# A gated linear attention and a star-ReLU feed-forward on one core: another order of the opening, and w_in cast in other pieces

## The chip, the cores and the metric

The kernel runs on one core of one Trainium2 chip. The metric is the device time of one execution in microseconds. Before the change three runs gave 196.47, 197.56 and 197.69 us; the median is 197.56.

## The reference

Two layers one after the other. The first is a recurrence over 768 steps for each of 4 batches and 8 heads, with a state of 48 by 48; the second takes its output, with the heads put side by side, as 3072 tokens of width 384.

```python
for t in range(S):                         # q, k, v, alpha: (4, 8, 768, 48)
    state = alpha[:, :, t, :, None] * state + einsum('bhd,bhe->bhde', k[:, :, t], v[:, :, t])
    y[:, :, t] = einsum('bhd,bhde->bhe', q[:, :, t], state)
x = y.transpose(0, 2, 1, 3).reshape(3072, 384)
h = x @ w_in                               # w_in: (384, 2048)
g = s * maximum(h, 0) ** 2 + b
out = g @ w_out                            # w_out: (2048, 384), out: (3072, 384) float32
```

## The kernel before

The 3072 tokens are cut into 24 blocks of 128, six to each batch. A block n goes through these steps, each a small function:

- `load(n)`: four DMAs on SP's queue, alpha, k, q, v, in this order, 192 KB each.
- `ln(n)` (L189, ACT): the logarithm of alpha, written to `la_sb`. `vcast(n)` (L192, POOL): v to bf16.
- `cum(n)`: the running sum of the logarithms as a matmul with a triangle of ones (L198, and four narrow ones, L201, for the total), and on ACT the exponentials `bi_sb` (L209), `b_sb` (L210) and `blast` (L212).
- `qk(n)` (DVE): `kb_sb` = k times `bi_sb` (L226) and `qb_sb` = q times `b_sb` (L227).
- `tr(n)`: eight transposes on PE (L232) and one copy by DVE to `qkT` (L237).
- `amat(n)`: eight matmuls (L247) give the scores within the block, and DVE masks them into `am_a` and `am_b` (L255).
- `yp(n)`: the output of the block from the state (`sd_sb`, L266) and from the scores (L275), the state's increment (L286), and on ACT the copy `y_bf` (L293). `st(n)`: the state's update, one DVE instruction (`t_sb`, L337 or L339) and two or three on POOL (L344, L348).
- `xt(n)`: three transposes of `y_bf` (L317) and ACT's copy into `xd_all` (L323).
- `mr(g, u)`: one 512-wide piece of the first matrix product of group g (L365) and its relu on ACT into a ring of eight buffers `r_sb` (L379). `sq(g, u)` (L386, DVE) squares it into `gt_all`. Group 0 holds blocks 0 and 1, so its pieces cover 256 columns of w_in; group 1 is block 2, group 2 is block 3, and their pieces cover 512 columns.
- `o(n, u)`: a quarter of the second product (L403).

Weights arrive as float32 and are cast on the chip. `win(i)` casts a quarter of w_in's 2048 columns in three instructions, one for each 128 rows: `cast_w_in(c0, c1, act)` gives the first `act` of them to ACT (L140) and the others to DVE (L142). `wout(i)` casts a quarter of w_out and multiplies it by s, on DVE (L146) or, for i = 1, on ACT (L154). `busy(n)` issues n matmuls whose result nobody reads (L179). `colsum` and `bias_sum` work on the bias.

Nothing is reordered by a scheduler. `at(pos, fn, ...)` collects the steps, and they are issued in the order of their positions; every engine takes its instructions in that order. The opening, up to block 4's `amat`, is a list written out by hand, which takes positions in steps of 0.1; the rest follows from formulas. SP's queue begins with the loads of blocks 0 to 3, then the four quarters of w_in, the four of w_out, and the loads of blocks 4 to 7. `cum` of the first four blocks writes the PSUM bank `h_ps[1]`, `xt` of the first three `h_ps[0]`; the first pieces of `mr` go round five banks.

Of the kernel before, what the change touches and what calls it, by code (L numbers as in the profile page):

```python
# [14 lines left out]
def kernel(  # L15
# [122 lines left out]
    def cast_w_in(c0, c1, act=1):  # L138
        for kk in range(act):
            nc.scalar.activation(out=w_in_bf[:, kk, c0:c1], in_=w_in_st[:, kk, c0:c1], func=AF.Copy)  # L140
        for kk in range(act, KT):
            nc.vector.tensor_copy(out=w_in_bf[:, kk, c0:c1], in_=w_in_st[:, kk, c0:c1])  # L142
# [307 lines left out]
    quarter = d_ff // 4  # L450
# [24 lines left out]
    def at(pos, fn, *args):  # L475
        events.append((pos, len(events), fn, args))
# [5 lines left out]
    def wout(i):  # L482
        cast_w_out(4 * i, 4 * i + 4, i == 1)

    def win(i):
        cast_w_in(i * quarter, (i + 1) * quarter, 2 if i == 0 else 1)

    def m(g, u):
        mp(g, u)
# [10 lines left out]

    for pos, what in enumerate(
        [
            (ln, 0), (vcast, 0), (cum, 0), (qk, 0), (spread,), (busy, 3), (tr, 0), (ln, 1), (busy, 1), (vcast, 1), (cum, 1), (amat, 0),
            (busy, 3), (yp, 0), (qk, 1), (st, 0), (busy, 1), (tr, 1), (xt, 0), (ln, 2), (busy, 2), (vcast, 2), (cum, 2), (amat, 1),
            (busy, 3), (yp, 1), (qk, 2), (st, 1), (busy, 1), (tr, 2), (xt, 1), (ln, 3), (busy, 2), (vcast, 3), (cum, 3), (amat, 2),
            (busy, 3), (yp, 2), (qk, 3), (st, 2), (busy, 1), (tr, 3), (xt, 2), (busy, 3), (amat, 3), (win, 0), (busy, 4), (yp, 3),
            (mr, 0, 0), (mr, 0, 1), (xt, 3), (mr, 1, 0), (win, 1), (sq, 0, 0), (mr, 0, 2), (mr, 0, 3), (mr, 1, 1), (win, 2), (sq, 0, 1),
            (sq, 1, 0), (mr, 2, 0), (mr, 2, 1), (win, 3), (st, 3), (sq, 0, 2), (sq, 0, 3), (mr, 0, 4), (mr, 0, 5), (wout, 0), (mr, 1, 2),
            (sq, 1, 1), (sq, 2, 0), (mr, 2, 2), (sq, 2, 1), (mr, 0, 6), (sq, 0, 4), (o, 0, 0), (wout, 1), (mr, 0, 7), (sq, 0, 5),
            (o, 1, 0), (mr, 1, 3), (sq, 1, 2), (o, 2, 0), (mr, 2, 3), (sq, 2, 2), (sq, 0, 6), (wout, 2), (sq, 0, 7), (o, 0, 1), (sq, 1, 3),  # L510
            (o, 1, 1), (sq, 2, 3), (ln, 4), (wout, 3), (o, 2, 1), (cum, 4), (o, 0, 2), (vcast, 4), (qk, 4), (o, 1, 2), (o, 2, 2), (colsum, 1),
            (o, 0, 3), (o, 1, 3), (tr, 4), (o, 2, 3), (o, 3, 0), (colsum, 2), (amat, 4),
        ]
    ):
        at(0.1 * pos, *what)
# [64 lines left out]
```

## Time and profile before

| | |
|---|---|
| runs | 196.47, 197.56, 197.69 us |
| profiled execution | 196.55 us, its span 194.8 us |
| PE busy | 180.9 us, 93% of the span |
| DVE, ACT, POOL busy | 150.5, 119.5, 61.4 us |
| DMA | 30.31 MB, mean 156 GB/s |
| costliest lines on PE | L365 71.1 us, L403 68.3 us |
| costliest line on ACT | L379 53.5 us |

The span is what the profiler saw on the core; the execution's own time is 1.75 us longer. "Idle before, and its releaser" names the time in which an engine stood still and the instruction that let it go on; on an engine that is not the bound such time costs nothing. Times in a timeline are in us from the span's start. Starts of successive instructions on one engine can be closer than their durations, because they overlap.

### The profile page before, as it was taken

To read this page: it belongs to the slowest core of one execution; us is meant where nothing else is said; L and a number is where in the kernel's file an instruction comes from. 1 tells how busy PE (TensorE), PEld (TensorE's weight loads), DVE (VectorE), ACT (ScalarE), POOL (GpSimd) and SP (SyncE) were. 2 spreads that over 40 slices of the span, in tenths; PEclk is the share of its full clock that TensorE was granted. 3 is DMA by queue.
4 is the path that set the end of the run, shared out by engine and by line. 5 is a ranking of instruction groups with operands and counts; after the bars stand their busy time and mean duration, and the time that the engine had idled before them with its cause. 6 is when DMAs were issued, how large, how long until landed. Compare 5 with 4: busy or idle time off the path is not lost.

```text
span 194.8 us, 6003 instructions
## 1 busy us (share of the span) xinstructions
PE 180.9 (93%) x2389; PEld 143.3 (74%) x2391; DVE 150.5 (77%) x294; ACT 119.5 (61%) x245; POOL 61.4 (32%) x96
## 2 busy tenths in 40 slices
PE   1977879999999999999999999999999999999994
PEld 1544459866777788778878888888877877877783
DVE  5367778657687788888887996878988988998532
ACT  3344567953677666766677676775675566654640
POOL 5154404021310515624500641642401565352000
PEclk9999999999999999999999999999999999999999
DMA  6999999999996484484958448759886948433212
GB/s 126 188 185 190 359 388 371 233 192 188 186 156 108 71 155 88 80 150 82 173 91 162 83 85 162 131 80 198 165 175 149 216 117 166 128 120 121 84 40 81
DMA packets 113453, 30.31 MB, mean 156 GB/s; under 512 B 106627, under 2 KB 111890, under 8 KB 113426
## 3 DMA queue, kind: packets, MB, share of 16 engines
q1 hardware_dynamic: 113422, 29.94, 74.3%
q8 instruction: 18, 0.29, 0.7%
q14 instruction: 9, 0.07, 0.1%
q10 hardware_dynamic: 4, 0.00, 0.0%
HBM read 25.19 MB, written 4.74 MB: 154 GB/s over the span
## 4 chain that ended last, share of the span: by engine, by line
PE 80%; DVE 4%; ACT 3%; issue 1%; ACTq 0%
PE h_ps L365 29%; PE o_ps L403 28%; PE ct_ps L232 5%; PE a_ps L247 3%; PE a_ps L403 3%; PE y_ps L275 2%; ACT r_sb L379 2%; PE h_ps L317 2%; PE ct_ps L198 2%; PE a_ps L426 1%; PE p_ps L286 1%; PE y_ps L266 1%; DVE gt_all L386 1%; DVE w_out_bf L146 1%; DVE am_b L255 1%
## 5 line engine op out<-in xcount | busy, mean ns | idle before, releaser
L379 ACT ACTIVATE r_sb<-h_ps 128x512 bf16<-128x512 f32 x90 | 53.5, 597 | 35.5 <-PE h_ps L365 33.2
L365 PEld LDWEIGHTS <-w_in_bf 128*128 128x128 bf16 x1104 | 67.9, 98 | 8.0 <-ACT w_in_bf L140 1.4
L365 PE MATMUL h_ps<-xd_all,w_in_bf 128*128 128x128 bf16 (+1 forms) x1044 | 71.1, 221 | 0.1
L403 PE MATMUL o_ps<-w_out_bf,gt_all 128*128 128x384 bf16 x336 | 68.3, 326 | 0.1
L386 DVE TENSOR_TENSOR gt_all<-r_sb 128x512 bf16<-128x512 bf16 x96 | 45.1, 482 | 26.5 <-ACT r_sb L379 25.8
L344 POOL TENSOR_TENSOR sd_sb<-t_sb,blast 48x192 bf16<-48x192 f32 x40 | 20.1, 503 | 91.8 <-DVE t_sb L339 53.9
L403 PEld LDWEIGHTS <-gt_all 128*128 128x128 bf16 x368 | 32.6, 98 | 16.0
L192 POOL CAST v_bf<-v_sb 128x384 bf16<-128x384 f32 x24 | 17.0, 712 | 24.2 <-DMA v_sb<-in_v_dram 20.7
L348 POOL TENSOR_TENSOR sc_sb<-t_sb,blast 112x384 f32<-112x384 f32 x16 | 22.0, 1372 | 1.3
L323 ACT ACTIVATE xd_all<-h_ps 128x384 bf16<-128x384 bf16 x23 | 11.3, 491 | 15.6 <-PE h_ps L317 15.6
L237 DVE COPY qkT<-ct_ps 112x1024 bf16<-112x1024 bf16 x24 | 16.4, 683 | 4.5 <-PE ct_ps L232 3.0
L255 DVE TENSOR_TENSOR am_a<-a_ps,mask 128x512 bf16<-128x512 f32 x24 | 16.4, 683 | 4.2 <-PE a_ps L247 4.1
L226 DVE TENSOR_TENSOR kb_sb<-k_sb,bi_sb 128x384 bf16<-128x384 f32 x24 | 13.8, 574 | 4.5 <-ACT bi_sb L209 4.5
L255 DVE TENSOR_TENSOR am_b<-a_ps,mask 128x512 bf16<-128x512 f32 x24 | 16.3, 680 | 0.0
L227 DVE TENSOR_TENSOR qb_sb<-q_sb,b_sb 128x384 bf16<-128x384 f32 x24 | 16.0, 668 | 0.0
L293 ACT ACTIVATE y_bf<-y_ps 128x384 bf16<-128x384 f32 x24 | 11.7, 489 | 5.6 <-PE y_ps L275 5.6
L189 ACT ACTIVATE la_sb<-al_sb 128x384 bf16<-128x384 f32 x24 | 12.4, 516 | 3.9 <-DMA al_sb<-in_alpha_dram 3.9
L232 PEld LDWEIGHTS <-qb_sb 128*112 128x112 bf16 x96 | 8.3, 133 | 5.3 <-DVE qb_sb L227 4.1
L209 ACT ACTIVATE bi_sb<-ct_ps 128x384 f32<-128x384 f32 x20 | 9.7, 486 | 2.3 <-PE ct_ps L201 1.3
L232 PE MATMUL ct_ps<-ident,qb_sb 128*112 128x128 bf16 x96 | 9.9, 227 | 0.9 <-DVE qb_sb L227 0.9
L210 ACT ACTIVATE b_sb<-ct_ps 128x384 f32<-128x384 f32 x20 | 9.9, 495 | 0.0
L275 PE MATMUL y_ps<-v_bf,am_b 128*128 128x48 bf16 x96 | 8.1, 184 | 1.7 <-DVE am_b L255 1.7
(75 smaller groups left out, 200.9 us busy)
## 6 DMA issues: line engine op xcount, KB each, us to landing
al_sb<-in_alpha_dram SPq DMA_DIRECT2D x24, 192.0 KB, 4.1
k_sb<-in_k_dram SPq DMA_DIRECT2D x24, 192.0 KB, 4.0
q_sb<-in_q_dram SPq DMA_DIRECT2D x24, 192.0 KB, 4.4
v_sb<-in_v_dram SPq DMA_DIRECT2D x24, 192.0 KB, 5.2
w_in_st<-in_moe_w_in_dram SPq DMA_DIRECT2D x4, 768.0 KB
w_out_st<-in_moe_w_out_dram SPq DMA_DIRECT2D x4, 768.0 KB, 12.8
out_dram<-w_in_st SPq DMA_DIRECT2D x14, 192.0 KB, 2.0
out_dram<-out_sb SPq DMA_DIRECT2D x9, 192.0 KB
```

What stands on the lines that cost most here:

```text
L192: nc.gpsimd.tensor_copy(out=v_bf[n % 3], in_=v_sb[n % NLD])
L226: nc.vector.tensor_tensor(out=kb_sb[n % 3][:, :, 0:48], in0=k_sb[n % NLD], in1=bi_sb[n % 2], op=ALU.mult)
L227: nc.vector.tensor_tensor(out=qb_sb[n % 2][:, :, 0:48], in0=q_sb[n % NLD], in1=b_sb[n % 3], op=ALU.mult)
L232: nc.tensor.transpose(out=t_ps[0:112, x, p, :], in_=t.rearrange("a h d -> a (h d)")[:, 128 * p : 128 * p + 112], identity=ident,)
L237: nc.vector.tensor_copy(out=qkT_sb[n % 2][0:112].rearrange("a x p t -> a (x p t)"), in_=t_ps[0:112].rearrange("a x p t -> a (x p t)"),)
L255: nc.vector.tensor_tensor(out=am_sb[e][n % 2], in0=a_ps[e], in1=mask4, op=ALU.mult)
L344: nc.gpsimd.tensor_tensor(out=sd[r, :, d], in0=t1_sb[r, :, d], in1=bl[r].to_broadcast([48, NP, 48]), op=ALU.mult)
L348: nc.gpsimd.tensor_tensor(out=sc_sb[0:112], in0=t1_sb[0:112], in1=bl[0:112].to_broadcast([112, NP, 96]), op=ALU.mult)
L365: nc.tensor.matmul(out=hp[:, jj * N : (jj + 1) * N], lhsT=w_in_bf[:, kk, 128 * j : 128 * (j + 1)], rhs=xd_sb[g][:, kk, 0:N], start=(kk == ...
L379: nc.scalar.activation(out=rs, in_=h_of.pop((g, u)), func=AF.Relu)
L386: nc.vector.tensor_tensor(out=gt_sb[g][:, u * 512 : (u + 1) * 512], in0=rs, in1=rs, op=ALU.mult)
L403: nc.tensor.matmul(out=op[:, 0:d_model], lhsT=gt_sb[g][:, j * N + t * C : j * N + (t + 1) * C], rhs=w_out_bf[:, j, :], start=(j == 0), sto ...
```

## The change

The list of the opening is written anew, and `win` works on units of 256 columns.

- `busy` ahead of `tr(0)` has two matmuls instead of three; the two ahead of `cum(2)` and of `cum(3)` become one, placed behind it; the four ahead of `yp(3)` become three.
- `amat(0)` is placed ahead of `cum(1)`.
- `ln(2)` is placed ahead of `xt(0)`, and `ln(3)` ahead of `xt(1)`.
- `win(i)` casts 256 columns with all three instructions on ACT; `win(i, 2)` casts 512, one instruction on ACT and two on DVE. The first quarter becomes `win(0)` ahead of `yp(3)` and `win(1)` behind it. The other three stay 512 wide and are placed among the first pieces of `mr`: the first of them between `mr(0,0)` and `mr(0,1)`, the next between `mr(0,2)` and `mr(0,3)`, the last between `mr(2,0)` and `mr(2,1)`.
- `ln(4)` and `cum(4)` are placed some steps earlier (`cum(4)` ahead of `o(2,1)`), and `tr(4)` ahead of `o(1,3)`.

On the engines: ACT has six casts of 256 columns and three of 512 instead of five of 512; DVE has six casts instead of seven; PE has four matmuls and their weight loads fewer; the orders of DVE, POOL and SP are otherwise the same.

```diff
-    def win(i):
-        cast_w_in(i * quarter, (i + 1) * quarter, 2 if i == 0 else 1)
+    def win(i, n=1):
+        cast_w_in(i * 256, (i + n) * 256, 3 if n == 1 else 1)
...
-            (ln, 0), (vcast, 0), (cum, 0), (qk, 0), (spread,), (busy, 3), (tr, 0), (ln, 1), (busy, 1), (vcast, 1), (cum, 1), (amat, 0),
-            (busy, 3), (yp, 0), (qk, 1), (st, 0), (busy, 1), (tr, 1), (xt, 0), (ln, 2), (busy, 2), (vcast, 2), (cum, 2), (amat, 1),
-            (busy, 3), (yp, 1), (qk, 2), (st, 1), (busy, 1), (tr, 2), (xt, 1), (ln, 3), (busy, 2), (vcast, 3), (cum, 3), (amat, 2),
-            (busy, 3), (yp, 2), (qk, 3), (st, 2), (busy, 1), (tr, 3), (xt, 2), (busy, 3), (amat, 3), (win, 0), (busy, 4), (yp, 3),
-            (mr, 0, 0), (mr, 0, 1), (xt, 3), (mr, 1, 0), (win, 1), (sq, 0, 0), (mr, 0, 2), (mr, 0, 3), (mr, 1, 1), (win, 2), (sq, 0, 1),
-            (sq, 1, 0), (mr, 2, 0), (mr, 2, 1), (win, 3), (st, 3), (sq, 0, 2), (sq, 0, 3), (mr, 0, 4), (mr, 0, 5), (wout, 0), (mr, 1, 2),
+            (ln, 0), (vcast, 0), (cum, 0), (qk, 0), (spread,), (busy, 2), (tr, 0), (ln, 1), (busy, 1), (vcast, 1), (amat, 0), (cum, 1),
+            (busy, 3), (yp, 0), (qk, 1), (st, 0), (busy, 1), (tr, 1), (ln, 2), (xt, 0), (vcast, 2), (cum, 2), (busy, 1), (amat, 1),
+            (busy, 3), (yp, 1), (qk, 2), (st, 1), (busy, 1), (tr, 2), (ln, 3), (xt, 1), (vcast, 3), (cum, 3), (busy, 1), (amat, 2),
+            (busy, 3), (yp, 2), (qk, 3), (st, 2), (busy, 1), (tr, 3), (xt, 2), (busy, 3),
+            (amat, 3), (win, 0), (busy, 3), (yp, 3), (win, 1),
+            (mr, 0, 0), (win, 2, 2), (mr, 0, 1), (xt, 3), (mr, 1, 0), (sq, 0, 0), (mr, 0, 2), (win, 4, 2), (mr, 0, 3), (sq, 0, 1), (mr, 1, 1),
+            (sq, 1, 0), (mr, 2, 0), (win, 6, 2), (mr, 2, 1), (st, 3), (sq, 0, 2), (sq, 0, 3), (mr, 0, 4), (mr, 0, 5), (wout, 0), (mr, 1, 2),
             (sq, 1, 1), (sq, 2, 0), (mr, 2, 2), (sq, 2, 1), (mr, 0, 6), (sq, 0, 4), (o, 0, 0), (wout, 1), (mr, 0, 7), (sq, 0, 5),
-            (o, 1, 0), (mr, 1, 3), (sq, 1, 2), (o, 2, 0), (mr, 2, 3), (sq, 2, 2), (sq, 0, 6), (wout, 2), (sq, 0, 7), (o, 0, 1), (sq, 1, 3),
-            (o, 1, 1), (sq, 2, 3), (ln, 4), (wout, 3), (o, 2, 1), (cum, 4), (o, 0, 2), (vcast, 4), (qk, 4), (o, 1, 2), (o, 2, 2), (colsum, 1),
-            (o, 0, 3), (o, 1, 3), (tr, 4), (o, 2, 3), (o, 3, 0), (colsum, 2), (amat, 4),
+            (o, 1, 0), (mr, 1, 3), (sq, 1, 2), (o, 2, 0), (mr, 2, 3), (sq, 2, 2), (sq, 0, 6), (ln, 4), (wout, 2), (sq, 0, 7), (o, 0, 1),
+            (sq, 1, 3), (o, 1, 1), (sq, 2, 3), (cum, 4), (wout, 3), (o, 2, 1), (o, 0, 2), (vcast, 4), (qk, 4), (o, 1, 2), (o, 2, 2),
+            (colsum, 1), (o, 0, 3), (tr, 4), (o, 1, 3), (o, 2, 3), (o, 3, 0), (colsum, 2), (amat, 4),
```

## The prediction

> **What bounds the kernel now.** I read the page first: shares, slices, releasers.
>
> ```profile
> span 194.8 us, 6003 instructions
> PE 180.9 (93%) x2389; PEld 143.3 (74%) x2391; DVE 150.5 (77%) x294; ACT 119.5 (61%) x245; POOL 61.4 (32%) x96
> ...
> PE   1977879999999999999999999999999999999994
> ...
> PEclk9999999999999999999999999999999999999999
> ```
>
> PE is busy 93% of the span, and only the first six slices of 4.87 us and the last show gaps. So microseconds can be won in the opening alone, and what the opening gains the end gets, because from there on PE's own work sets the pace. The table of stretches confirms it (columns: stretch, its length, busy us and instructions of PE, PEld, DVE, ACT, POOL, then PEclk, DMA share, GB/s):
>
> ```profile
> 14.00:19.00 5.00, 3.71 (x47) 2.42 (x46) 3.51 (x6) 2.33 (x6) 2.28 (x5) 1.00 1.30 182
> 26.00:28.00 2.00, 2.00 (x27) 1.78 (x24) 1.11 (x5) 1.67 (x4) 0.00 (x0) 1.00 1.05 400
> 28.00:30.00 2.00, 0.76 (x9) 0.64 (x8) 1.91 (x6) 1.25 (x3) 0.00 (x0) 1.00 1.06 377
> 32.00:36.00 4.00, 3.87 (x55) 3.53 (x53) 3.67 (x7) 4.00 (x9) 0.59 (x1) 1.00 1.07 360
> 100.00:150.00 50.00, 49.88 (x701) 41.16 (x700) 42.70 (x81) 33.74 (x71) 15.15 (x20) 1.00 0.72 132
> ```
>
> Blocks 1 to 3 take about 5 us each, PE idle for over a quarter of it and filled with dummy matmuls besides. At 28 to 30 us PE is idle for 1.24 us. At 100 to 150 us it idles for 0.12 of 50.
>
> Then the timeline of the opening, for what each gap waits on (start, us, engine, line, operation; in brackets the idle time before and what ended it):
>
> ```profile
> 16.48 0.55 DVE L227 TENSOR_TENSOR qb_sb<-q_sb,b_sb 128x384 bf16<-128x384 f32 x1
> ...
> 17.77 0.69 DVE L237 COPY qkT<-ct_ps 112x1024 bf16<-112x1024 bf16 x1 [0.28 <-PE ct_ps L232]
> 17.94 0.49 ACT L323 ACTIVATE xd_all<-h_ps 128x384 bf16<-128x384 bf16 x1 [1.05 <-PE h_ps L317]
> ...
> 18.32 0.52 ACT L189 ACTIVATE la_sb<-al_sb 128x384 bf16<-128x384 f32 x1
> ...
> 18.89 0.32 PE L198 MATMUL h_ps<-la_sb,U_bf 128*128 128x384 bf16 x1 [0.56 <-ACT la_sb L189]
> ...
> 19.30 0.40 PE L247 MATMUL a_ps<-qkT 48*128 48x128 bf16 x8
> ```
>
> This is block 2. Its qkT is done at 18.46, yet its amat (L247) starts at 19.30. In PE's order it stands behind cum(3), which waits for ln(3), which stands on ACT behind the copy of xt(1). Block 1 is the same (xt copy 12.87, ln 13.26, cum 13.82, amat 14.24). The second gap:
>
> ```profile
> 28.61 0.64 ACT L140 ACTIVATE w_in_bf<-w_in_st 128x512 bf16<-128x512 f32 x1
> ...
> 29.30 0.83 PE L365 MATMUL a_ps<-xd_all,w_in_bf 128*128 128x256 bf16 x6 [1.24 <-ACT w_in_bf L140]
> ```
>
> Here mr(0,2) waits for ACT's part of the cast of the second quarter of w_in, which stands behind two relus, the copy of xt(3) and a third relu.
>
> **When the data lands.** Moving work earlier pays only up to its load, so I need landings that the trace mostly hides. In the first 16 us a load lands 4.7 us after its issue starts: al(1) 3.52 to 8.24, v(1) 6.69 to 11.42, v(2) 10.94 to 15.64, each ending an idle wait. By that, al(2) lands at 7.72+4.7=12.4, al(3) at 16.7, k(3) 17.7, q(3) 18.75. v(3) is seen at 20.75. A quarter of w_in or w_out is 0.786 MB, 2.1 us at 377 GB/s, so counted from 20.75 the quarters of w_in land at 22.8, 24.9, 27.0, 29.0 and those of w_out at 31.1, 33.2, 35.3, 37.4. Before, their casts began at 23.43, 25.6, 27.6, 29.1 and 31.83 without idling: consistent, and upper bounds. Then 0.197 MB a load at 190 GB/s, 1.03 us: al(4) 38.4, k(4) 39.5, q(4) 40.5, v(4) 41.6; v(4) ended a wait at 41.72. SP's order is unchanged and waits for no compute here, so landings stay.
>
> **The change, part by part.**
>
> *ln ahead of xt, amat ahead of cum(1).* One block's circle, by start times of block 2: am_a to kb 1.20 (14.67, 15.87), kb to qb 0.61, qb to transposes 0.60, to qkT 0.69, to the earliest amat 0.75 (22.87, 23.62), to am_a 0.43: 4.28 us instead of 5.06. Block 0: amat no longer waits for cum(1), 7.97+0.75=8.72 instead of 9.23. am_a 9.2, kb(1) 10.4 (bi(1), now behind amat, at 10.2), qb(1) 10.85 (q(1) landed at 10.3; one step 0.46 as at 10.94 and 11.40), transposes 11.45, qkT 12.15. ln(2) waits for al(2): 12.4 to 12.92, cum(2) 12.97. From cum to amat 0.42 (13.82, 14.24), and one dummy matmul that now stands between, 0.22: amat(1) 13.6, for 14.24. Two stood ahead of cum, inside its wait, so dropping them gives nothing. The copy of xt(0) moves behind ln(2), but PE finishes that transpose about then anyway. Block 2: 13.6+4.28=17.9 for the qkT, and 17.2+0.05+0.64=17.9 by ln(3): amat(2) 17.9, for 19.30. Block 3: 22.2, for 23.62. v(3) is cast by 21.25 and sd(2) follows on POOL to 22.35, in time for yp(3). Gain 1.42, and mr(0,0) starts at 25.75-1.42=24.33. If al(2) and al(3) landed only where ln started before (13.26, 18.32), the dummy between would cost 0.22 a block, in all -0.2: these are the two ends. I take 1.42, since 4.7 us was seen three times.
>
> *win(0) and win(1) in halves, all on ACT.* ACT pieces of 512 and 384 start 0.52 and 0.385 apart back to back; by that slope 256 takes 0.25. Three from 22.8 end at 23.65, hidden behind amat(3) and yp(3); even from 23.43 they end at 24.3, just in time. win(1) follows the y_bf copy (24.42): 24.8 to 25.66. mr(0,0) ends at 24.98, so PE waits 0.7 for mr(0,1) at 25.7: this is the new wait, priced in. DVE loses one cast of 0.42 behind am_b(3), which bounded nothing.
>
> *The later casts.* On ACT win(2,2) now stands ahead of the second relu: done 26.6 against mr(0,2) at 27.2. The next, done by 29.0 and 31.0, come before mr(0,4) and mr(0,6). So the 1.24 us gap goes. From 25.7 PE has 11 groups of 0.67 and one transpose of 0.17 up to mr(0,6): 33.25, for 35.61. ACT needs the same time (relu 0.48, cast 0.52): done with relu(1,2), which frees mr(0,6)'s bank, at 32.95. w_out's first cast ends by 31.15+1.58=32.7, o(0,0) needs it at 33.95. Gain so far 2.36: 1.42 and 1.24 and 0.4 of smaller waits, less 0.7.
>
> *ln(4), cum(4), tr(4) earlier.* cum(4) moves ahead of o(2,1), to 42.16-2.36-0.65=39.15. relu(2,3) ends at 38.55 and al(4) lands at 38.4, so la is ready at 39.1: no stall, and no margin. If al(4) landed as late as its use before (40.91), everything behind cum(4) on PE (o(2,1), o(0,2) and on) would wait 2.3 us. qb(4) at 40.7 has its q, tr(4) is at 42.9. Later loads are needed 2.4 us earlier; by row v(5), v(7) land at 46.0 and 54.6 and yp(5), yp(7) are behind 52 and 60. Nothing is late.
>
> [...]
>
> Sum: the profiled execution took 196.55 (span 194.8 and 1.75 around it); less 2.36, 194.2. The runs were 196.47, 197.56, 197.69, so that execution is at the low end; halfway to the median adds 0.45: **194.6**.
>
> **Rivals.**
> *cum(4) waits for al(4)*, 0.10. For: no margin, and a landing worked out, not seen. Against: the same reckoning meets v(4). At half the bound, 1.2 us is given back: 195.8; at all of it 197.0.
> *The loads pace blocks 1 to 3*, 0.10. Front -0.2, the mr stage still +0.94: 196.2. Against: the three equal landings.
> *ACT is the bound from 24 to 33 us*, 0.12. It carries three more casts of 256; between 32 and 36 it was already busy 4.00 of 4.00. If that eats the 0.94, the front remains: 195.6.
> *PE's clock falls*, 0.10, the slower side. Four of 27 dummy matmuls go. Eight transposes took 0.89 from 6.83 and 0.44 from 12.01, although PEclk reads full throughout: PE was half as fast before 8 us. Should it stay so until the dense matmuls, a circle would be 4.28+0.44+0.43, and the PE pieces ahead of amat (xt 0.17, cum 0.42, dummy 0.22) would double past qkT's 0.75, 0.8 more: 5.96, for 5.06. Three blocks, less the head start of 0.5, put mr(0,0) 2.2 late; less 0.94: 198.3. It decides if PE's share of work falls. Against: by the sum a block has 3.71-0.22 us of PE work in 4.28, 82% instead of 73%.
> [...]
>
> **How the numbers follow.** Forecast 0.58. A difference within 1% of the median is about what this measurement can't tell from none; faster by over 1% is below 195.6. Of the forecast's chance 0.53 lies there, and half of ACT's as bound: 0.58 or so. Slower is the clock, 0.10; the rest, 0.32, is between. The range ends below at a gain of 3.2 from the low runs (mr(0,1) without its wait): 193.3; above at al(4)'s bound, 197.1.
>
> **What would show it.** ln(2) starting at 12.4 after a wait for DMA; amat at 13.6, 17.9, 22.2; mr(0,0) at 24.3 with a gap of 0.7 behind it and none near 29; cum(4) near 39.2 without a wait for la. The forecast is wrong if ln(3) starts later than 17.5, if PE's dummy matmuls after 12 us start more than 0.3 apart, or if PE stands idle for over 0.5 us ahead of cum(4).

## The result, and the profile after

The change takes 194.89 us in the median of four runs (194.75 to 195.42), against 197.01 for the kernel before in runs beside it (196.46 to 197.69). The ratio is 0.9895, with a 95% interval of 0.9863 to 0.9926: faster by about 1%, near the forecast of 194.6. The profiled execution took 195.03, 1.52 less than that of before (196.55).

The page, with PE's share and slices:

```profile
span 193.3 us, 5998 instructions
...
PE 182.0 (94%) x2385; PEld 144.5 (75%) x2387; DVE 150.5 (78%) x293; ACT 119.9 (62%) x249; POOL 62.0 (32%) x96
...
PE   0898889999899999999999999999999999999994
```

The table of stretches, for the same windows as before (stretch, length, busy us and instructions of PE, PEld, DVE, ACT, POOL, PEclk, DMA share, GB/s):

```profile
14.00:19.00 5.00, 3.97 (x50) 2.60 (x52) 3.40 (x7) 2.60 (x8) 2.10 (x4) 1.00 1.32 192
...
26.00:28.00 2.00, 1.84 (x21) 1.37 (x21) 0.76 (x3) 2.00 (x6) 0.00 (x0) 1.00 1.05 403
28.00:30.00 2.00, 2.00 (x29) 1.87 (x26) 1.56 (x6) 2.00 (x6) 0.00 (x0) 1.00 1.07 381
...
32.00:36.00 4.00, 3.98 (x47) 3.38 (x46) 4.00 (x9) 3.67 (x8) 1.78 (x2) 1.00 1.06 360
...
100.00:150.00 50.00, 49.88 (x705) 41.29 (x703) 42.55 (x81) 34.07 (x72) 16.49 (x22) 1.00 0.76 136
```

The gap at 28 to 30 us is gone (PE 2.00 of 2.00, for 0.76), a small one stands at 26 to 28, and the steady part is as it was. The timeline of the blocks, where the prediction expected ln(2) at 12.4, amat(1) at 13.6 and amat(2) at 17.9:

```profile
12.22 0.63 PE L232 MATMUL ct_ps<-ident,qb_sb 128*112 128x128 bf16 x4
12.53 0.52 ACT L189 ACTIVATE la_sb<-al_sb 128x384 bf16<-128x384 f32 x1 [0.32 <-DMA al_sb<-in_alpha_dram]
12.65 0.63 PE L232 MATMUL ct_ps<-ident,kb_sb 128*112 128x128 bf16 x4
...
13.40 0.53 PE L198 MATMUL h_ps<-la_sb,U_bf 128*128 128x384 bf16 x1
...
14.59 0.61 PE L247 MATMUL a_ps<-qkT 48*128 48x128 bf16 x8 [0.38 <-issue]
...
15.13 0.83 PE L179 MATMUL o_ps<-mask,U_bf 128*128 128x512 bf16 x3
...
17.35 0.52 ACT L189 ACTIVATE la_sb<-al_sb 128x384 bf16<-128x384 f32 x1
...
18.17 0.33 PE L198 MATMUL h_ps<-la_sb,U_bf 128*128 128x384 bf16 x1
...
18.95 0.40 PE L247 MATMUL a_ps<-qkT 48*128 48x128 bf16 x8
```

ln(2) came at 12.53 behind a wait for its load, as forecast. But amat(1) came at 14.59, later than before the change (14.24), and its matmuls took 0.61 instead of 0.40. The transposes took 0.63 a group of four instead of 0.43 and 0.39. (The 0.38 of idle time shown ahead of amat(1) is the dummy's: this trace has only its weight load, at 13.98; the trace of e7, whose list is the same there, has the matmul too, 0.59 long.) Two lines of the profile of before show the other speed:

```profile
8.82 0.32 PE L198 MATMUL h_ps<-la_sb,U_bf 128*128 128x384 bf16 x1 [0.46 <-ACT la_sb L189]
...
14.24 0.40 PE L247 MATMUL a_ps<-qkT 48*128 48x128 bf16 x8
```

So PE ran at about half speed until about 15 us in the change (the three dummies at 9.92 took 1.44, those at 15.13 0.83), and was fast from 8.8 on before (0.82 for three dummies at 9.56). PEclk reads 1.00 between 9 and 14 us in both, so the durations are the thing to read. Set against before, amat(2) came 0.35 earlier and amat(3) 0.52, and the casts added 0.88.

| start of | before | forecast | the change | e10 (below) |
|---|---|---|---|---|
| amat(1) | 14.24 | 13.6 | 14.59 | 13.55 |
| amat(2) | 19.30 | 17.9 | 18.95 | 18.01 |
| amat(3) | 23.62 | 22.2 | 23.10 | 22.16 |
| mr(0,0) | 25.75 | 24.33 | 25.23 | 24.29 |
| mr(0,6) | 35.61 | 33.25 | 34.21 | 33.27 |
| cum(4) | 42.16 | 39.15 | 40.12 | 39.19 |
| profiled execution | 196.55 | 194.2 | 195.03 | 194.07 |

### The profile page after: what moved, and what is told of

Same layout as the page of the kernel before. It is cut to its first block, busy times and chain, and to the rows that moved or that the text cites. A ratio compares the mean times of both kernels' runs of the same rounds, so it can differ in the third digit from the quotient of the medians.

```text
span 193.3 us, 5998 instructions
## 1 busy us (share of the span) xinstructions
PE 182.0 (94%) x2385; PEld 144.5 (75%) x2387; DVE 150.5 (78%) x293; ACT 119.9 (62%) x249; POOL 62.0 (32%) x96
## 4 chain that ended last, share of the span: by engine, by line
PE 83%; DVE 2%; ACT 2%; issue 1%; ACTq 0%
PE h_ps L365 30%; PE o_ps L403 29%; PE ct_ps L232 5%; PE a_ps L247 3%; PE a_ps L403 3%; PE y_ps L275 2%; PE h_ps L317 2%; PE ct_ps L198 2%; PE a_ps L426 1%; PE y_ps L266 1%; PE p_ps L286 1%; PE o_ps L365 1%; PE a_ps L365 1%; ACT r_sb L379 1%; ACT y_bf L293 1%
## 5 line engine op out<-in xcount | busy, mean ns | idle before, releaser
L386 DVE TENSOR_TENSOR gt_all<-r_sb 128x512 bf16<-128x512 bf16 x96 | 46.3, 499 | 25.2 <-ACT r_sb L379 24.4
L344 POOL TENSOR_TENSOR sd_sb<-t_sb,blast 48x192 bf16<-48x192 f32 x40 | 21.0, 526 | 87.8 <-DVE t_sb L339 55.8
L237 DVE COPY qkT<-ct_ps 112x1024 bf16<-112x1024 bf16 x24 | 16.4, 684 | 4.9 <-PE ct_ps L232 3.4
L255 DVE TENSOR_TENSOR am_a<-a_ps,mask 128x512 bf16<-128x512 f32 x24 | 16.4, 684 | 3.7 <-PE a_ps L247 3.7
L255 DVE TENSOR_TENSOR am_b<-a_ps,mask 128x512 bf16<-128x512 f32 x24 | 16.4, 682 | 0.0
L227 DVE TENSOR_TENSOR qb_sb<-q_sb,b_sb 128x384 bf16<-128x384 f32 x24 | 15.5, 644 | 0.0
L189 ACT ACTIVATE la_sb<-al_sb 128x384 bf16<-128x384 f32 x24 | 12.4, 516 | 4.3 <-DMA al_sb<-in_alpha_dram 4.3
L247 PE MATMUL a_ps<-qkT 48*128 48x128 bf16 x192 | 10.0, 226 | 0.8 <-issue 0.4
```

The costliest lines, as they stand in the source:

```text
L227: nc.vector.tensor_tensor(out=qb_sb[n % 2][:, :, 0:48], in0=q_sb[n % NLD], in1=b_sb[n % 3], op=ALU.mult)
L237: nc.vector.tensor_copy(out=qkT_sb[n % 2][0:112].rearrange("a x p t -> a (x p t)"), in_=t_ps[0:112].rearrange("a x p t -> a (x p t)"),)
L247: nc.tensor.matmul(out=a_ps[e][:, p, :], lhsT=qkT[r0 : r0 + 48, 1, p, :], rhs=qkT[r0 : r0 + 48, 0, p, :], start=True, stop=True,)
L255: nc.vector.tensor_tensor(out=am_sb[e][n % 2], in0=a_ps[e], in1=mask4, op=ALU.mult)
L344: nc.gpsimd.tensor_tensor(out=sd[r, :, d], in0=t1_sb[r, :, d], in1=bl[r].to_broadcast([48, NP, 48]), op=ALU.mult)
L386: nc.vector.tensor_tensor(out=gt_sb[g][:, u * 512 : (u + 1) * 512], in0=rs, in1=rs, op=ALU.mult)
```

## The experiments

Theory A: the order is worth what the sum says, and a late start of PE's full speed took the rest. Theory B: the order of the blocks is itself worth only 0.5 us. All ratios are to the kernel before in runs taken beside it. Behind a time stands the range of its runs, behind a ratio its 95% interval. For each experiment one execution was profiled, and the times of single steps are from that one.

**e1, the blocks' part alone.** The first three lines of the new list, and three dummies ahead of yp(3); all else as before.

> Only the blocks' part of the change: ln ahead of xt, amat(0) ahead of cum(1), and the four dummy matmuls fewer; casts of w_in, and ln(4), cum(4), tr(4), as before. By the prediction's sum it gains 1.42 us on before (amat(3) at 22.2, mr(0,0) at 24.3), and the 1.24 us gap ahead of mr(0,2) stays. Theory A, that PE's late waking took 0.9 us of this part in the profiled execution of the change: between 0.5 us (amat(1) near 14.6 with its eight matmuls taking 0.61) and 1.4 us (amat(1) near 13.6, 0.40), by when PE gets fast in the execution looked at. Theory B, that the new order itself is worth only 0.5 us, whatever the clock: 0.5 us with amat(1) late although its matmuls take 0.40.

Measured: 195.45 (195.21 to 196.15), ratio 0.9916 (0.9884 to 0.9947). In the profile amat(1) came at 14.24, amat(3) at 22.54, mr(0,0) at 24.68, 1.07 earlier than before; PE got fast at about 13.9 (a group of four transposes 0.63 at 12.56, amat(1) 0.40 at 14.24). mr(0,6) followed 9.86 us behind mr(0,0), just as before (25.75, 35.61), and the wait for the cast stayed. That lies between A's ends and against B's 0.5; amat(1)'s matmuls took 0.40, but the transposes ahead of it were slow (0.63 for 0.39 to 0.43).

**e2, the casts alone.** The new `win` and its places; list lines of the blocks and of the tail as before.

> Only the casts' part: win in halves and in the new places; blocks 1 to 3 and their dummy matmuls as before, ln(4), cum(4), tr(4) as before. By the prediction's sum 0.94 us gained on before: a new gap of 0.7 us ahead of mr(0,1), none of 1.24 us ahead of mr(0,2), mr(0,6) 0.9 earlier. The rival that ACT becomes the bound in this stage: less than 0.3 us gained, with relus back to back on ACT and PE waiting for them. If the two parts add up, e1 and e2 together give the change's 2.1 us.

Measured: 195.80 (195.66 to 196.51), ratio 0.9933 (0.9911 to 0.9956). On PE:

```profile
25.79 2.16 PE L365 MATMUL h_ps<-xd_all,w_in_bf 128*128 128x256 bf16 x12
27.95 0.83 PE L365 MATMUL o_ps<-xd_all,w_in_bf 128*128 128x128 bf16 x12
28.62 0.82 PE L365 MATMUL a_ps<-xd_all,w_in_bf 128*128 128x256 bf16 x6
```

mr(0,0) and mr(0,1) take 2.16 together instead of 1.47 (the new wait), and the third line follows without the 1.24 us gap. mr(0,6) comes 8.98 behind mr(0,0), 0.88 less than before; the sum had 0.94. ACT as the bound of this stage is ruled out: behind that line PE has no wait for a cast or a relu up to mr(0,6). By landmarks the parts make the change: 8.98 again in the change, 9.86 in e1. By medians they do not add (1.98 and 1.63 less than 197.43, the change 2.1 less than 197.01), which is discussed below.

**e3, dummy matmuls ahead of everything.**

```diff
+    def warm(n):
+        for i in range(n):
+            nc.tensor.matmul(out=o_ps[:, 0:128], lhsT=U_bf, rhs=U_bf, start=True, stop=True)
...
+            (warm, 26), (ln, 0), ...
```

> The changed kernel with 26 dummy matmuls of 128 columns put ahead of everything on PE, where it otherwise stands idle until 4.4 us. [...] Theory B (the order itself): amat(3) stays near 23.1 and the time near 194.9.

Measured: 195.18 (194.99 to 195.33), ratio 0.9896 (0.9870 to 0.9922): no faster than the change, where theory A with PE fast early has the sum's 194.2. PE was busy from 1.36 us, yet slow all the same:

```profile
1.36 2.95 PE L190 MATMUL o_ps<-U_bf 128*128 128x128 bf16 x26 [1.36 <-POOL U_bf masks.py:66]
...
12.60 0.63 PE L236 MATMUL ct_ps<-ident,kb_sb 128*112 128x128 bf16 x4
...
14.02 0.38 PE L179 MATMUL o_ps<-mask,U_bf 128*128 128x512 bf16 x1
14.33 0.40 PE L251 MATMUL a_ps<-qkT 48*128 48x128 bf16 x8
```

It got fast at about 14.0. So the experiment did not do what it was made for, and could not tell A from B: early work alone did not bring the full speed forward.

**e4, no dummies at all.** Every `(busy, n)` taken out of the list.

> The changed kernel with none of its 23 dummy matmuls, so that their effect is seen as a whole. If they keep PE fast (theory A): PE stays at half speed through blocks 1 to 3 (transposes 0.87 from the first to the last start instead of 0.45), mr(0,0) comes at 26 to 28, and the kernel is 1 to 3 us slower than the change. If a block's own matmuls suffice, PE gets fast at about the same time as in the change, and the time is within 0.3 us of it.

Measured: 197.45 (196.27 to 197.92), ratio 1.0006 (0.9982 to 1.0031). By the ratios (1.0006 and 0.9895) the 23 dummies are worth 2.2 us, by the medians (197.45 and 194.89, whose kernels before differ by 0.4) 2.6: as much as the whole change, and what theory A expected. PE stays slow to the dense part:

```profile
13.85 0.61 PE L247 MATMUL a_ps<-qkT 48*128 48x128 bf16 x8
19.03 0.61 PE L247 MATMUL a_ps<-qkT 48*128 48x128 bf16 x8
23.84 0.61 PE L247 MATMUL a_ps<-qkT 48*128 48x128 bf16 x8 [0.47 <-DVE qkT L237]
26.41 2.76 PE L365 MATMUL h_ps<-xd_all,w_in_bf 128*128 128x256 bf16 x12
29.28 1.49 PE L365 MATMUL o_ps<-xd_all,w_in_bf 128*128 128x128 bf16 x12
```

The last line, 1.49 for twelve matmuls that take 0.83 when fast, shows half speed as late as 30 us.

**e5, the breaks in front of tr(0) and amat(0) filled too.** On e3:

```diff
-            (warm, 26), ... (spread,), (busy, 2), (tr, 0), (ln, 1), (busy, 1), (vcast, 1), (amat, 0), (cum, 1),
+            (warm, 26), ... (spread,), (busy, 3), (tr, 0), (ln, 1), (busy, 2), (vcast, 1), (amat, 0), (cum, 1),
```

> The changed kernel with the 26 early dummy matmuls and two more that close the gaps in front of tr(0) and amat(0), so that PE is busy without a break from 1.4 to 9 us. [...] Theory A2 (work put in early does not count, whatever its length): amat(1) at 14.2 to 14.6 as before, the time 194.8 to 195.4.

Measured: 195.04 (194.86 to 195.32), ratio 0.9902 (0.9881 to 0.9923). PE was fast early, against theory A2, and yet the time was A2's. It was fast from 4.4 us (cum(0) 0.32 at 4.38, for 0.48 at 4.43 in the change), 3.0 us behind its first matmul: amat(1) 13.41, amat(2) 17.87, amat(3) 22.02, mr(0,0) 24.15, mr(0,6) 33.13, all within 0.2 of the prediction's sum. So theory B falls. But the won 1.1 us was gone by amat(4), at 46.13 against 46.21 in the change:

```profile
4.38 0.32 PE L202 MATMUL h_ps<-la_sb,U_bf 128*128 128x384 bf16 x1
...
39.47 0.52 ACT L193 ACTIVATE la_sb<-al_sb 128x384 bf16<-128x384 f32 x1 [0.93 <-DMA al_sb<-in_alpha_dram]
40.05 0.32 PE L202 MATMUL ct_ps<-la_sb,U_bf 128*128 128x384 bf16 x1 [0.84 <-ACT la_sb L193]
```

ln(4) waited until 39.47 for alpha(4), and PE 0.84 us for it: the prediction's rival at cum(4). The change in its own profile reached cum(4) too late to meet that wait; in e3, which reached it a little earlier, PE waited 0.18. That the load of alpha(4) takes back what the earlier full speed wins is theory C.

**e6, the kernel before with the same dummies.**

> The kernel before with the same: 26 early dummy matmuls and one more ahead of cum(1). [...]

Measured: 196.66 (195.98 to 197.03), ratio 0.9977 (0.9961 to 0.9992). Its profile (196.46) became fast at 8.7 (L205's four matmuls 0.49 at 4.72, 0.32 at 8.87), much as that of before did at 8.8, and its landmarks lie within 0.2 of that profile's (mr(0,0) 25.65 for 25.75). Whether the higher runs of before (up to 197.8) are executions with a late start of full speed, which this run was to tell, is not settled: all profiles of the old order that were taken, e2's among them, show an early one, and e6's runs still spread over a microsecond.

**e7, the tail as before.** ln(4), cum(4) and tr(4) at their old places, all else as in the change.

> The changed kernel with ln(4), cum(4) and tr(4) where they were before. The prediction gave this part nothing: within 0.2 us of the change. If cum(4)'s place ahead of o(2,1) made PE wait, or if an earlier block 4 shortened the way to the steady part, the time differs by more than 0.4 us, and the start of yp(4)'s first matmul with it.

Measured: 194.67 (194.23 to 195.29), ratio 0.9885 (0.9862 to 0.9907); the unchanged change beside it, e8, 194.54. Nothing, as forecast; amat(4) at 46.15 (46.21 in the change). PE got fast as late as in the change here (amat(1)'s matmuls 0.61), so this says nothing of an early full speed, with which e5's cum(4) met its wait.

**e8, the change once more.**

> The changed kernel once more, for a second profile and more runs beside the others. If its runs differ by when PE gets fast, this profile's front (amat(1) between 13.6 and 14.6) goes with its time: an amat(1) before 14.0 with a time below 194.8, one at 14.5 or later with 195.0 to 195.4.

Measured: 194.54 (194.26 to 195.12), ratio 0.9876 (0.9854 to 0.9899). PE got fast near 13 us (transposes 0.60 at 12.59, those of xt(0) 0.34 at 13.02); amat(1) 13.98, mr(0,0) 24.74, cum(4) 39.63 without a wait, and the execution took 194.54. So the profile's front goes with its time: full speed 2 us earlier, 0.5 us less.

**e9, cum(4) later.** On e5:

```diff
-            (sq, 1, 3), (o, 1, 1), (sq, 2, 3), (cum, 4), (wout, 3), (o, 2, 1), (o, 0, 2), (vcast, 4), ...
+            (sq, 1, 3), (o, 1, 1), (sq, 2, 3), (wout, 3), (o, 2, 1), (o, 0, 2), (cum, 4), (vcast, 4), ...
```

> e5's kernel (PE kept busy from 1.4 to 9 us) with cum(4) placed behind o(0,2) instead of ahead of o(2,1), two groups of 0.65 us later on PE. Theory C (in e5 PE woke early, but the won time was lost again at cum(4), where PE stood 0.84 us for la(4), which waited 0.93 us for the load of alpha(4)): PE has work until la(4) is there, no wait ahead of cum(4), amat(4) near 45.3 instead of 46.13, and the time 0.7 to 0.9 us below e5's in executions in which PE wakes as early: near 194.1. Rival (something behind, such as the load of v(4) or PE's total work, takes it in any case): amat(4) or yp(4) as late as in e5, the time near 195.0.

Measured: 194.43 (194.10 to 196.01), ratio 0.9884 (0.9851 to 0.9917). Three of six runs are at the expected 194.1 to 194.3, but the profiled one took 195.50, for another reason:

```profile
17.69 0.52 ACT L193 ACTIVATE la_sb<-al_sb 128x384 bf16<-128x384 f32 x1 [1.47 <-DMA al_sb<-in_alpha_dram]
...
18.26 0.32 PE L202 MATMUL h_ps<-la_sb,U_bf 128*128 128x384 bf16 x1 [0.86 <-ACT la_sb L193]
...
19.10 0.61 PE L251 MATMUL a_ps<-qkT 48*128 48x128 bf16 x8
```

alpha(3) landed at 17.7, over a microsecond later than in e5 (ln(3) 16.40) or e10, PE stood still for it, and fell back to half speed (amat(2)'s matmuls 0.61, three dummies 1.46 at 19.65). Here PEclk says so too, with 0.50 between 19 and 21 us, and the page's row, as e12's does, while those of before and of the change read 9 throughout:

```profile
PEclk9999799999999999999999999999999999999999
```

Two more of the prediction's rivals, in one execution. The wait ahead of cum(4) was gone, but with mr(0,0) at 25.72 it could not have come.

**e10, alpha(4) loaded earlier.** On e5:

```diff
     for j in range(0, NJ, 4):
+        if j == 12:
+            nc.sync.dma_start(out=al_sb[4], in_=src(alpha, 4))
         load_w_out(j, j + 4)
```

(and block 4's later load without alpha).

> e5's kernel with one load moved on SP: alpha(4) is loaded ahead of the last quarter of w_out instead of behind it, cum(4) stays ahead of o(2,1). Theory C: alpha(4) lands about 2 us earlier, near 37.4, the last quarter of w_out 1 us later, which the cast at 38.9 still meets or misses by little; no wait ahead of cum(4), amat(4) near 45.3, the time near 194.1. Rival: if the wait at cum(4) was not alpha(4)'s landing, PE waits there still, and the time stays near 195.0.

Measured: 194.11 (194.05 to 194.41), ratio 0.9853 (0.9829 to 0.9877). PE was fast from 10.8 (two dummies 1.06 at 7.85, 0.60 at 10.41).

```profile
38.53 0.81 PE L407 MATMUL a_ps<-w_out_bf,gt_all 128*128 128x384 bf16 x4
38.58 0.52 ACT L193 ACTIVATE la_sb<-al_sb 128x384 bf16<-128x384 f32 x1
...
39.19 0.33 PE L202 MATMUL ct_ps<-la_sb,U_bf 128*128 128x384 bf16 x1
```

ln(4) and cum(4) start without a wait, amat(4) at 45.27: theory C holds, its rival falls. Every landmark is within 0.15 of the sum, and the time within 0.15 of it too (194.07 for 194.2). Of the versions tried it has the lowest median. That it is faster than the change is likely but not shown: the change's nine runs lie at 194.26 to 195.42, and the intervals of the ratios overlap. Against e5 they do not (0.9881 to 0.9923).

**e11, the blocks' part with the dummies of e5.**

> The blocks' part alone (as e1) with PE kept busy from 1.4 to 9 us: the prediction's term of 1.42 us with the clock taken out, against e6, the kernel before with the same dummies (196.66 median). By the prediction: amat(3) 1.3 to 1.45 earlier than e6's 23.52, the gap of 1.24 ahead of mr(0,2) still there, cum(4) reached no earlier than 40.5 and so without a wait for alpha(4), the time 1.4 below e6's: near 195.25. Theory B (the order is worth 0.5): near 196.2.

Measured: 196.09 (195.17 to 196.43), ratio 0.9939 (0.9918 to 0.9960). PE was fast from 4.6 (cum(0) 0.32 at 4.57), amat(1) came at 13.64, but in the profiled execution (196.38) alpha(3) was late:

```profile
17.98 0.52 ACT L193 ACTIVATE la_sb<-al_sb 128x384 bf16<-128x384 f32 x1 [1.68 <-DMA al_sb<-in_alpha_dram]
```

amat(2) at 19.20, amat(3) at 23.35: only 0.17 earlier than e6's. So the median misses the expectation. Four of the nine runs lie at 195.2 to 195.7, near the expected 195.25; that those had alpha(3) in time was not seen, since one execution is profiled.

**e12, both e9's and e10's edits.**

> Both, e9's later cum(4) and e10's earlier load of alpha(4). Theory C: only one of them is needed, so no faster than the better of e9 and e10 by more than 0.2 us. If the loads of k(4) and q(4) were the next wait behind alpha(4), this one would show it: DVE waiting for a load ahead of kb(4) or qb(4).

Measured: 195.49 (194.39 to 196.01), ratio 0.9914 (0.9887 to 0.9942). Its profile repeats e9's: PE waits 1.22 us for la(3), and cum(3) and amat(2) are slow (0.48, 0.61). It is no test of the two edits, and kb(4) and qb(4) could not show a next wait. Other traces show it: q(4), for which DVE waited in e10 (0.17) and in e8:

```profile
41.81 0.56 DVE L227 TENSOR_TENSOR qb_sb<-q_sb,b_sb 128x384 bf16<-128x384 f32 x1 [0.57 <-DMA q_sb<-in_q_dram]
```

It cost PE nothing: amat(4) comes 20.98 behind mr(0,0) in both, as in the change.

## Why the prediction was right, and where its steps were off

The direction, the size and both parts of the gain were right. That the median came within 0.3 of the forecast is in part luck: for the profiled execution the sum gave 194.2 and 195.03 came, because PE got fast late, and the 0.45 that the forecast added for the spread of before's runs covered half of that.

- **ln ahead of xt, 1.42 us.** The mechanism and the size are right, on a condition: PE fast by 11 us, and alpha(3) in time. Then e5 and e10 meet each landmark, and their amat(3) comes 1.50 and 1.36 earlier than in e6, the old order with early dummies (23.52). From amat(1) to amat(2) it is 4.46 us, bounded by ln(3)'s load (waited for 0.33 in both) and a longer qb on DVE (0.86 in e10, the next 0.55), then 4.15, for 4.28. In the profiled execution of the change only 0.52 came.
- **PE's speed, mis-sized.** The sum took PE as fast from 8.8 us, as it was before. The late start cost 1.0: transposes (0.63 a group for 0.43 and 0.39), cum (0.53 for 0.32) and the dummy in front of amat (0.59 in e7 for 0.38) all took longer, and amat(1) came at 14.59 for 13.6. The rival was priced for half speed all the way to the dense part (198.3); that was seen only with no dummies (e4, 197.45). One dummy fewer ahead of tr(0) and a break ahead of amat(0) stand in the change where PE became fast in the profile of before. That they moved the start is likely: it lies at 13 to 15 us in all five profiles of the new order without these filled (the change, e1, e3, e7, e8), and at 8.7 to 9.0 in the three of the old order (before, e2, e6). It was not tried singly, and the sign that was to show a slow PE could not: only one dummy stands between 12 us and the full speed at 15. The other two signs did not come either (ln(3) at 17.35, no wait ahead of cum(4)).
- **What starts the full speed** was not shown. The traces have it depend on more than the amount of work: with the same 26 matmuls at the head it came at 4.4 (e5), 4.6 (e11), about 5.0 (e9, e12), 8.7 (e6), 10.8 (e10) and 14.0 us (e3), and e5, e9, e10 and e12 have the same order on PE up to there. In e5 it came 3.0 us behind PE's first matmul, in e10, with the same steps, 9.4 behind. What ends it was not shown either: e9 fell back at about 18.6 us (a dummy 0.57 for 0.38), after idle stretches of 0.72 and 0.86 us within 2.4 us, and e11 kept 0.38 at 18.89 behind 0.72 and 1.07.
- **The halves of w_in, 0.94 us.** Right: 0.88 in the change, in e2 and in e10. The pieces of 256 are 0.305 us apart (three in 1.02, the last 0.41), not 0.25 as the straight line from 512 and 384 gave. The difference cost nothing, because mr(0,1) can start on the first piece (PE's weight loads waited for these casts three times, 0.8 us in all); the new wait came to 0.66 (mr(0,0) to xt(3) 2.00, less two groups of 0.67) for 0.72.
- **alpha(4), 38.4.** Landed at 39.4 in e5, a microsecond later than reckoned. The reckoning was early for other loads of block 4 in the change too, without early dummies: q(4) landed at 41.8 in e8 (reckoned 40.5), v(4) at 42.4 there and at 42.9 in the change's first profile (41.6). When alpha(4) landed in the change is not seen, only that it was there by 39.5 and by 39.0 (e8). It cost nothing, because PE's late start had already made everything later by half a microsecond to one; with PE fast early in e5 it cost 0.84. So one error hid the other, and the forecast's 194.2 was met where both were mended (e10, 194.07).
- **alpha(3), 16.7.** Right in the change, e5, e8 and e10 (ln(3) no later than 17.4, where it waited 16.4 and 16.5), wrong in e9, e11 and e12 (17.7 to 18.0). These three have the early dummies, and slower loads go with those: e5, e9, e10 and e11, which have them, moved 134, 141, 125 and 137 GB/s between 17 and 19 us; before, the change and e8, without them, moved 180, 200 and 210. So a late alpha(3) may come of the experiment, and is not shown for the change itself. But e5 and e10 have the low rate with alpha(3) in time, so the rate is not the cause alone; that stays open. One row of before could have warned that 4.7 us does not always hold: v(3) was issued at 15.09 and ended a wait at 20.75, 5.66 later.
- **Later loads, nothing late.** Right for PE: from 60 us on it has no more than 0.12 us of idle time in any of the wide stretches up to 185 us, as before.
- **The medians.** Before's runs were centred at 197.0 to 197.4 and its profile at 196.55, so medians gain more (2.1 to 2.5) than the profiles (1.5); why is open. The forecast added 0.45, half of that distance (half of 1.01 is 0.5), to the sum. The change's profile lay 0.14 from its own median, so with PE fast early the sum alone would have been nearer: e10's median is 194.11. The bound of al(4), 2.3 on 194.6, makes 196.9 and not the 197.0 and 197.1 that are written; nothing hangs on it.

## What to carry to other kernels

Before a step is moved forward in an opening, write down when each load lands that it and its next three neighbours need; a gain in front can be lost at the next load, as 0.84 us was here at alpha(4), and one load moved in its queue gave it back. Read PE's speed from the duration of one repeated group, such as 0.40 or 0.61 for the same eight matmuls, not from a clock row, which read full in the change beside the 0.61, and count dummy matmuls as part of the schedule: these 23 are worth 2.2 to 2.6 us. Compare landmarks of profiles, not only medians, when two parts are to be added.

## What was not expected of the hardware

- PE's full speed began anywhere from 4.4 (e5) to 15 us (the change) in kernels that differ by a few dummies. With 26 extra matmuls of 3 us at the head it began at 14.0 in one (e3) and, with two more behind them, at 4.4 in another (e5); and e10, with the same opening on PE as e5, began at 10.8.
- It was lost again behind idle stretches of 1.02, 0.72 and 0.86 us in e9 (amat(2) 0.61), and of 1.05, 0.72 and 1.22 in e12 (0.61), while e11, with 1.23, 0.72 and 1.07, kept it (0.40).
- The same load at the same place in the queue (alpha(3)) landed between 16.4 (e5) and 18.0 us (e12). Between 17 and 19 us the load rate was 125 to 141 GB/s in four profiles with the early dummies (e5, e9, e10, e11), and 180 to 210 in three without (before, the change, e8).
